# Two DMA queues for the KV stream of a decode block: V by SyncE, the next step's K by ScalarE

## The chip, the cores and the metric

One core of a Trainium2 chip runs the kernel; its other cores do nothing for it. The metric is the device time of one execution in microseconds (us). A core has TensorE (PE; its weight loads are shown apart as PEld), VectorE (DVE), ScalarE (ACT), GpSimd (POOL) and SyncE (SP, which only waits and issues), and 16 DMA engines that move data between the memory outside (HBM) and the on-chip SBUF. A DMA is issued by an engine, stands in that engine's DMA queue, and is cut into rows, one for each SBUF partition; with 128 partitions each of the 16 DMA engines carries eight rows of it.

## The reference, cut to what matters

One decode step for a batch of 2. `x` is normalised; an attention branch over a cache of 4096 positions is multiplied by a gate from a feed-forward branch and added to `x`:

```python
xn = _layernorm(x)                                   # (2, 1, 448)
q = (xn @ wq) -> (2, 16 heads, 1, 256)               # 16 query heads, 8 KV heads
scores = einsum("bhqd,bhkd->bhqk", q, k) * 256**-0.5 # k: (2, 8, 4096, 256), each KV head serves 2 query heads
o = einsum("bhqk,bhkd->bhqd", softmax(scores), v)    # v: the same shape as k
s = o.reshape(2, 1, 16 * 256) @ wo                   # (2, 1, 448)
g = silu(((xn @ w_gate) * (xn @ w_up)) @ w_down)     # inner width 1792
return x + s * g
```

All is float32. K and V are 67 MB each and are read once; with the weights the kernel reads 158.5 MB.

## The kernel before, in words

Batch and KV head make 16 steps; step `i` is head `i // 2`, batch `i % 2`. For one step K is 4 MB, laid out as 128 rows (partitions) of 32 KB, and so is V. The host joins V of step `i` and K of step `i + 1` into one tile `vk[i]` with rows of 64 KB (`ROW` = 8192 floats is one half of a row). These tiles go through `ring`, a pool of two SBUF buffers of 64 KB per partition. The weights go through `slot`, a pool with one buffer.

All large DMAs are issued by SyncE, at L68 in the helper `issue(n)`, which takes the next `n` transfers of a list `todo`. The list's order is written out by hand: `wq0` (half of wq), `first` (K of step 0, which takes a whole ring buffer), `vk[0]`, `wgu` (w_gate and w_up), `vk[1]`, `vk[2]`, `wd` (w_down), `vk[3]`, `vk[4]`, `wq1`, `vk[5]` to `vk[8]`, `wo`, `vk[9]` to `vk[13]`, then `last0` (K of step 15 and V of step 14, as two DMAs) and `last1` (V of step 15 and the last part of wo, as seven). A DMA into a buffer waits on SyncE until all that read the buffer's former contents is done, and what stands behind it on SyncE waits with it. Step `i` in the loop issues `vk[i + 2]`, whose buffer held `vk[i]`; before it, it issues the weight tile that is next, if one is due.

Ahead of the loop, the first three transfers are issued; ScalarE issues two small DMAs (`x`, L90, 3.5 KB, and `xo`, L94, 3.5 KB); VectorE normalises x (L107 to L117), and `xnT` is ready at L122. `query(0)` (L147, L150) multiplies it with `wq0`, VectorE transposes the result to `qT` (L159), `scores(0)` (L212) is computed from `first`, `issue(2)` follows (wgu and `vk[1]`), then `softmax` (L218 to L233) and `over` (L240 to L242).

The loop's body for step `i`, in program order, is this:

```python
        values(i, p[0], o)          # 32 matmuls on V of step i, L249
        ss = scores(i + 1)          # 32 matmuls on K of step i + 1, L212, and two maxima on VectorE, L213
        issue(1 + (i + 1 in weights))
        nc.scalar.activation(ob[...], o, AF.Copy, scale=p[1])     # L300
        p = softmax(*ss)            # VectorE, PE and two exponentials on ScalarE, L231
```

After four of the steps a piece of other work follows, when its weight tile is there: `ffn_in` (step 0, wgu), `ffn_out` (step 2, wd), `query(1)` (step 4, wq1), `project` (step 8, wo). These free the `slot` buffer for the next weight tile. Behind the loop come the last two steps, the rest of the projection (L276, L282), the gate and the addition (L351, L352) and the output's DMA (L353).

An engine runs its instructions in program order; Tile's semaphores hold an instruction back until what it needs is there. Below, `V3` is V of step 3 and `K4` is K of step 4; both are halves of `vk[3]`.

Of the kernel before, what the change touches and what calls it, by code (L numbers as in the profile page):

```python
# [22 lines left out]
ROW = 8192  # L23
# [14 lines left out]
def gated_decode_block(ctx: ExitStack, tc: tile.TileContext, x, xo, first, vk, last0, last1, wq, wo, wgu, wd, out):  # L38
    nc = tc.nc
# [7 lines left out]
    def bank(name="s", bufs=3):  # L47
        return psum.tile([128, 512], F32, name=name, bufs=bufs)
# [5 lines left out]
    loaded = {}  # L54
    todo = []

    def issue(n=1):
        for names, src, cuts in todo[:n]:
            weight = names[0].startswith("w")
            if weight:  # L60
                t = slot.tile([128, PART], F32, name="slot", align_bytes=512)
            else:
                t = ring.tile([128, 2 * ROW], F32, name="ring", align_bytes=512)
            width = ROW if not weight else PART // len(names)
            for i, name in enumerate(names):
                loaded[name] = t[:, i * width:(i + 1) * width]
            for lo, hi in zip(cuts, cuts[1:]):
                nc.sync.dma_start(t[:, lo:hi], src[:, lo:hi])  # L68
        del todo[:n]

    def plan(names, src, cuts=None):
        todo.append((names.split(), src, cuts or [0, src.shape[1]]))
# [8 lines left out]
    plan(f"k{LAST + 1} v{LAST}", last0, [0, ROW, 2 * ROW])  # L81
    plan(f"v{LAST + 1} wo2", last1, [0, 4096, 7168, *(ROW + i * D for i in (0, 2, 6, 7, 8))])
    issue(3)


    def early():
# [68 lines left out]
    def query(h):  # L155
        ps = bank()
        rows(ps, loaded[f"wq{h}"], 512)
        for r in range(REP):
            nc.vector.transpose(qT[h][:, :, :, :, r, :].rearrange("p b g d j -> p (g d) b j"),  # L159
                                ps[:, r * 256:(r + 1) * 256])  # L160
# [6 lines left out]
    def lift(ps):  # L167
        t = work.tile([128, D], F32, name="h")
        nc.scalar.copy(t, ps[:, :D])
        return t  # L170
# [6 lines left out]
    def ffn_in():  # L177
        pp = []
        for w in ("wg", "wu"):
            ps = bank()  # L180
            rows(ps, loaded[w], FC)
            pp.append(ps)
        g = work.tile([128, FC], F32, name="h")
        nc.scalar.copy(g, pp[0][:, :FC])
        h = work.tile([128, FC], F32, name="h")
        nc.vector.tensor_mul(h, pp[1][:, :FC], g)
        nc.vector.transpose(hT.rearrange("p i m -> p (i m)"), h)

    def ffn_out():
        ps = bank()  # L190
        for i in range(14):
            t = i % NT
            nc.tensor.matmul(ps[W * t:W * (t + 1), :D], hT[:, i], loaded["wd"][:, i * D:(i + 1) * D],
                             start=i < NT, stop=i >= 14 - NT)
        y = bank()
        spread(lift(ps), y, True, True)
        e = work.tile([128, D], F32, name="h")[:, :SL]
        nc.scalar.activation(e, y[:, :SL], AF.Sigmoid)
        nc.vector.tensor_mul(gate, y[:, :SL], e)


    def scores(i):
        g, b = divmod(i, B)
        k = loaded[f"k{i}"].rearrange("p (h d c n) -> p h d c n", h=2, d=2, c=NT)
        q = qT[g // 4][:, b, g % 4].rearrange("p d r j -> p d (r j)")
        m = work.tile([128, 4], F32, name="m")
        ss = []
        for h in range(2):
            s = bank()
            for d in range(2):  # L210
                for c in range(NT):
                    nc.tensor.matmul(s[W * c:W * (c + 1), :], q[:, d], k[:, h, d, c, :], start=d == 0, stop=d == 1)  # L212
            nc.vector.tensor_reduce(m[:, h:h + 1], s, axis=AX.X, op=OP.max)  # L213
            ss.append(s)
        return ss, m

    def softmax(ss, m):
        nc.vector.tensor_max(m[:, 2:3], m[:, 0:1], m[:, 1:2])  # L218
        sm = bank("sm", 1)
        nc.tensor.transpose(sm[:1, :128], m[:, 2:3], ident)  # L220
        mx = work.tile([1, NT, W], F32, name="mx", bufs=1)
        nc.vector.tensor_reduce(  # L222
            mx, sm[:1, None, :128].rearrange("p o (c j) -> p o j c", c=NT).to_broadcast([1, NT, W, NT]),
            axis=AX.X, op=OP.max)
        nc.tensor.transpose(sm[:, 128:129], mx.rearrange("p c j -> p (c j)"), one)  # L225
        nc.vector.tensor_scalar(m[:, 3:4], sm[:, 128:129], -1.0 / 16, None, op0=OP.mult)  # L226
        su = work.tile([128, 4], F32, name="su")
        pT = []
        for h in range(2):
            p = work.tile([128, 512], F32, name="p")  # L230
            nc.scalar.activation(p, ss[h], AF.Exp, bias=m[:, 3:4], scale=1.0 / 16, accum_out=su[:, h:h + 1])  # L231
            t = work.tile([128, 512], F32, name="pT", bufs=4)
            nc.vector.transpose(t, p)  # L233
            pT.append(t)
        return pT, su, sm

    def over(p):

        pT, su, sm = p
        nc.vector.tensor_add(su[:, 2:3], su[:, 0:1], su[:, 1:2])  # L240
        nc.tensor.matmul(sm[:, 130:131], add_head.rearrange("p a r j -> p (a r j)"), su[:, 2:3], start=True, stop=True)  # L241
        nc.vector.reciprocal(su[:, 3:4], sm[:, 130:131])  # L242
        return pT, su[:, 3:4]

    def values(i, pT, o, lo=0, hi=KB):

        for e in range(lo, hi):
            h, t, at = e // 8, e % NT, e % 8 * 2 * W
            nc.tensor.matmul(o[W * t:W * (t + 1), :], pT[h][:, at:at + 2 * W:2],  # L249
                             loaded[f"v{i}"][:, e * 512:(e + 1) * 512], start=e < NT, stop=e >= KB - NT)  # L250

    def combine(ob, n):

        cb = bank("cb", 1)
        src = ob.rearrange("p s (e d c k) -> p s e d c k", e=2, d=2, c=NT)
        for e in range(2):
            for c in range(NT):
                nc.tensor.matmul(cb[W * c:W * (c + 1), :n * 64], add_blocks[:, e].rearrange("p r j -> p (r j)"),  # L258
                                 src[:, :n, e, :, c, :], start=e == 0, stop=e == 1)
        return cb  # L260
# [6 lines left out]
    def turn(oT, cb, g, b, n):  # L267
        nc.vector.transpose(oT[:, g:g + n, :, :, DUP * b:DUP * (b + 1)].rearrange("p g d r j -> p (g d) r j"), cb)
# [4 lines left out]
    def project(oT, first, lo, hi):  # L273
        for i in range(lo, hi):
            t = i % NT
            nc.tensor.matmul(wide[W * t:W * (t + 1), :D], heads(oT, i, first),  # L276
                             loaded["wo"][:, i * D:(i + 1) * D], start=i < NT, stop=i >= LATE - NT)
# [11 lines left out]
    oT2 = const.tile([128, 1, 2, REP, W], F32)  # L289
    ss = scores(0)  # L290
    issue(2)
    p = over(softmax(*ss))
    for i in range(LAST):
        g, b = divmod(i, B)
        o = bank("o", 1)
        values(i, p[0], o)
        ss = scores(i + 1)

        issue(1 + (i + 1 in weights))
        nc.scalar.activation(ob[:, b * 4 + g if g < 4 else b * 3 + g - 4], o, AF.Copy, scale=p[1])  # L300
        if i == LAST - 1:
            cb = combine(ob, 6)
        p = softmax(*ss)
        if i < LAST - 1:
            p = over(p)
        if i == 7:
            cb = combine(ob, 8)
            for n in range(B):
                turn(oT0, cb[:, n * 256:(n + 1) * 256], 0, n, 4)
            ob = work.tile([128, 8, 512], F32, name="ob", bufs=1)  # L310
        if i in weights:
            if i == 0:
                ffn_in()
            if i == 2:
                ffn_out()
            if i == 4:
                query(1)
            if i == 8:
                project(oT0, 0, 0, EARLY)
# [6 lines left out]
    t = lift(wide)  # L326
# [71 lines left out]
```

## Time and profile before

| | |
|---|---|
| median of 3 runs | 377.5 us (377.33 to 377.6) |
| the profiled execution | 377.77 us, span 375.5 us |
| PE busy | 200.2 us, 53% of the span |
| PEld, DVE, ACT, POOL busy | 60.8, 72.4, 39.9, 1.2 us |
| SyncE's DMA queue (q1) | 158.54 MB, 97.9% of the span on 16 engines |
| ScalarE's DMA queue (q10) | 20 packets, 0.01 MB |
| instruction fetches (q8) | 11 packets, 0.18 MB |
| read from HBM | 158.54 MB, 422 GB/s over the span |
| granted TensorE clock, mean | 0.773 |

The page gives each engine's busy time, the span in 40 slices with the busy share in tenths, the DMA queues, and the chain of work that ended last. The trace behind it answers for single lines, stretches and DMA records. Times of day in it are microseconds from the start of the span. A row of the timeline is: start, duration, engine, line, operation, output and input, count, and in brackets how long the engine had been idle and what ended that.

### The profile page before, as it was taken

How to read it: one execution, taken by the hardware profiler on the slowest of the kernel's cores; microseconds unless marked ns; L12 is line 12 of the kernel's file. 1: busy time of each engine (PE TensorE's matmuls, PEld its weight loads, DVE VectorE, ACT ScalarE, POOL GpSimd, SP SyncE). 2: the span in 40 equal slices, each digit the busy share in tenths (PEclk: the TensorE clock that was granted, in tenths of full speed). 3: DMA queues.
4: the chain of work that ended last, by engine and by line, in shares of the span. 5: the costliest groups of instructions: out<-in, count | busy, mean ns of one | idle time of the engine just before them, and what ended most of it. 6: DMA issues, size and time to landing. Idle time of an engine off the chain costs nothing.

```text
span 375.5 us, 3325 instructions
## 1 busy us (share of the span) xinstructions
PE 200.2 (53%) x1440; PEld 60.8 (16%) x1440; DVE 72.4 (19%) x176; ACT 39.9 (11%) x87; POOL 1.2 (0%) x7
## 2 busy tenths in 40 slices
PE   0661648083752918539183758523637282809764
PEld 0110112021210202102021212100112121202222
DVE  3013040104030030300304031300212112210520
ACT  1001010001012020100101010100100101010220
POOL 1000000000000000000000000000000000000000
PEclk9966697667788776687867789765958685968999
DMA  8999999999999999999999999999999999999993
GB/s 334 438 471 391 436 452 447 447 435 389 429 440 442 447 403 443 440 447 426 442 434 440 433 416 408 463 447 433 435 440 421 440 426 419 442 412 436 415 417 139
DMA packets 4241, 158.74 MB, mean 423 GB/s; under 512 B 514, under 2 KB 772, under 8 KB 1156
## 3 DMA queue, kind: packets, MB, share of 16 engines
q1 hardware_dynamic: 4208, 158.54, 97.9%
q8 instruction: 11, 0.18, 0.2%
q10 hardware_dynamic: 20, 0.01, 0.0%
q14 instruction: 2, 0.02, 0.0%
HBM read 158.54 MB, written 0.01 MB: 422 GB/s over the span
## 4 chain that ended last, share of the span: by engine, by line
DMA 79%; PE 19%; SPq 1%; issue 0%; DVE 0%
DMA ring<-vk 68%; PE o L249 11%; PE s L212 8%; DMA ring<-last 6%; DMA ring<-first 5%; SPq L68 1%; PE acc L282 0%; DVE h L351 0%; DVE h L352 0%
## 5 line engine op out<-in xcount | busy, mean ns | idle before, releaser
L249 PE MATMUL o<-ring,pT 128*32 128x512 f32 x480 | 80.9, 835 | 85.4 <-DMA ring<-vk 84.8
L212 PE MATMUL s<-ring,qT 128*32 128x512 f32 x512 | 60.8, 616 | 3.4 <-DMA ring<-first 3.4
L213 DVE TENSOR_REDUCE m<-s 128x1 f32<-128x512 f32 x32 | 22.1, 691 | 209.1 <-PE s L212 209.0
L249 PEld LDWEIGHTS o<-ring,pT 128*32 128x32 f32 x480 | 20.1, 147 | 137.6 <-issue 110.9
L231 ACT ACTIVATE p<-s,m 128x512 f32<-128x512 f32 x32 | 21.7, 683 | 97.6 <-DVE m L226 97.6
L300 ACT ACTIVATE ob<-o,su 128x512 f32<-128x512 f32 x14 | 9.6, 688 | 196.0 <-PE o L249 196.0
L241 PE MATMUL sm<-su,add_head 128*128 128x1 f32 x32 | 8.6, 336 | 38.2 <-DVE su L240 38.2
L233 DVE STREAM_TRANSPOSE pT<-p 128x512 f32<-128x512 f32 x32 | 22.1, 711 | 15.7 <-ACT p L231 15.7
L212 PEld LDWEIGHTS s<-ring,qT 128*32 128x32 f32 x512 | 17.5, 114 | 43.4 <-issue 39.2
L147 PE MATMUL s<-slot,xnT 128*32 128x512 f32 (+1 forms) x96 | 16.9, 860 | 7.1 <-DMA slot<-wq 5.1
L241 PEld LDWEIGHTS sm<-su,add_head 128*128 128x128 f32 x32 | 7.2, 279 | 40.5 <-DVE su L240 40.3
L222 DVE TENSOR_REDUCE mx<-sm 1x128 f32<-1x512 f32 x16 | 10.8, 678 | 8.3 <-PE sm L220 8.3
L220 PE MATMUL sm<-ident,m 128*1 128x128 f32 x16 | 4.3, 269 | 15.1 <-DVE m L218 15.1
L225 PE MATMUL sm<-one,mx 1*128 1x1 f32 x16 | 3.5, 218 | 12.3 <-DVE mx L222 12.3
L276 PE MATMUL wide<-slot,oT 128*32 128x448 f32 x48 | 7.7, 797 | 0.0
L147 PEld LDWEIGHTS s<-slot,xnT 128*32 128x32 f32 x96 | 3.9, 150 | 16.2 <-issue 16.2
L231 ACT ACTIVATION_READ_ACCUMULATOR p<-s,m 128x1 f32 x32 | 6.3, 196 | 0.0
L220 PEld LDWEIGHTS sm<-ident,m 128*1 128x1 f32 x16 | 1.3, 79 | 29.1 <-issue 23.1
L258 PE MATMUL cb<-ob,add_blocks 128*32 128x64 f32 (+2 forms) x64 | 5.6, 476 | 0.3 <-ACT ob L339 0.3
L249 PE MATMUL wide<-ring,pT 128*32 128x512 f32 x32 | 4.2, 600 | 2.2 <-DMA ring<-last 2.2
L242 DVE RECIPROCAL su<-sm 128x1 f32<-128x1 f32 x16 | 2.7, 169 | 11.8 <-PE sm L241 11.8
L225 PEld LDWEIGHTS sm<-one,mx 1*128 1x128 f32 x16 | 2.1, 133 | 15.7 <-DVE mx L222 15.7
(57 smaller groups left out, 46.1 us busy)
## 6 DMA issues: line engine op xcount, KB each, us to landing
ring<-last SPq DMA_DIRECT2D x2, 4096.0 KB, 26.3
slot<-wq SPq DMA_DIRECT2D x2, 3584.0 KB, 23.5
slot<-wgu SPq DMA_DIRECT2D x1, 6272.0 KB, 38.8
slot<-wo SPq DMA_DIRECT2D x1, 5376.0 KB
ring<-first SPq DMA_DIRECT2D x1, 4096.0 KB, 20.5
slot<-wd SPq DMA_DIRECT2D x1, 3136.0 KB
ring<-last SPq DMA_DIRECT2D x1, 2048.0 KB
ring<-last SPq DMA_DIRECT2D x1, 1536.0 KB, 18.7
```

Source lines behind the costliest of these rows:

```text
L147: nc.tensor.matmul(ps[W * c:W * (c + 1), :n], xnT[:, k, :], block(NT * k + c), start=k == 0, stop=False)
L212: nc.tensor.matmul(s[W * c:W * (c + 1), :], q[:, d], k[:, h, d, c, :], start=d == 0, stop=d == 1)
L213: nc.vector.tensor_reduce(m[:, h:h + 1], s, axis=AX.X, op=OP.max)
L220: nc.tensor.transpose(sm[:1, :128], m[:, 2:3], ident)
L222: nc.vector.tensor_reduce(mx, sm[:1, None, :128].rearrange("p o (c j) -> p o j c", c=NT).to_broadcast([1, NT, W, NT]), axis=AX.X, op=OP.max)
L225: nc.tensor.transpose(sm[:, 128:129], mx.rearrange("p c j -> p (c j)"), one)
L231: nc.scalar.activation(p, ss[h], AF.Exp, bias=m[:, 3:4], scale=1.0 / 16, accum_out=su[:, h:h + 1])
L233: nc.vector.transpose(t, p)
L241: nc.tensor.matmul(sm[:, 130:131], add_head.rearrange("p a r j -> p (a r j)"), su[:, 2:3], start=True, stop=True)
L249: nc.tensor.matmul(o[W * t:W * (t + 1), :], pT[h][:, at:at + 2 * W:2], loaded[f"v{i}"][:, e * 512:(e + 1) * 512], start=e < NT, stop=e >= ...
L276: nc.tensor.matmul(wide[W * t:W * (t + 1), :D], heads(oT, i, first), loaded["wo"][:, i * D:(i + 1) * D], start=i < NT, stop=i >= LATE - NT)
L300: nc.scalar.activation(ob[:, b * 4 + g if g < 4 else b * 3 + g - 4], o, AF.Copy, scale=p[1])
```

## The change

Of each `vk` tile SyncE now issues only the V half, as a DMA of 128 rows of 32 KB. The K half goes on a list, and `issue_second()` issues it from ScalarE, into the same ring buffer. In the loop `issue_second()` stands behind the `ob` copy (L300) and ahead of the softmax; ahead of the loop it stands behind the two calls of `issue`, the first of which comes before ScalarE's DMAs of `x` and `xo`. Weights, `first`, `last0` and `last1` stay as they are. The layout in HBM is the same: each half row is read from the same 64 KB row as before.

```diff
+    second = []
+
+    def issue_second():
+        for t, src in second:
+            nc.scalar.dma_start(t[:, ROW:], src[:, ROW:])
+        second.clear()
+
     def issue(n=1):
         for names, src, cuts in todo[:n]:
...
             for i, name in enumerate(names):
                 loaded[name] = t[:, i * width:(i + 1) * width]
+            if names[0][0] == "v" and names[-1][0] == "k":
+                second.append((t, src))
+                cuts = [0, ROW]
             for lo, hi in zip(cuts, cuts[1:]):
                 nc.sync.dma_start(t[:, lo:hi], src[:, lo:hi])
         del todo[:n]
...
     issue(3)
+    issue_second()
...
     ss = scores(0)
     issue(2)
+    issue_second()
     p = over(softmax(*ss))
     for i in range(LAST):
...
         issue(1 + (i + 1 in weights))
         nc.scalar.activation(ob[:, b * 4 + g if g < 4 else b * 3 + g - 4], o, AF.Copy, scale=p[1])
+        issue_second()
         if i == LAST - 1:
             cb = combine(ob, 6)
         p = softmax(*ss)
```

## The prediction

> **What bounds the kernel now.** I read the page first: slices, queues, the chain.
>
> ```profile
> DMA  8999999999999999999999999999999999999993
> ...
> q1 hardware_dynamic: 4208, 158.54, 97.9%
> ...
> DMA 79%; PE 19%; SPq 1%; issue 0%; DVE 0%
> ```
>
> SyncE's queue q1 keeps the 16 DMA engines busy for 97.9% of the span. What is missing lies before the first row (about 2 us) and behind the last (some 5 us), not in the middle. So a transfer that arrives earlier shortens nothing by itself: the end moves only if the rows pass faster, or if the engines run dry. The chain's PE parts are covered by the next tile's transfer. Now the timeline, tile by tile (start, duration, what):
>
> ```profile
> 3.24 0.61 DVE L107 TENSOR_REDUCE st<-pT 2x1 f32<-2x448 f32 x1 [2.25 <-DMA pT<-x]
> 12.16 5.30 PE L147 MATMUL s<-slot,xnT 128*32 128x512 f32 x24 [5.09 <-DMA slot<-wq]
> ...
> 21.85 6.44 PE L212 MATMUL s<-ring,qT 128*32 128x512 f32 x32 [3.39 <-DMA ring<-first]
> ...
> 28.35 21.94 SPq L68 DMA_DIRECT2D ring<-vk  x2
> ...
> 189.24 6.37 PE L249 MATMUL o<-ring,pT 128*32 128x512 f32 x32 [4.80 <-DMA ring<-vk]
> ...
> 208.55 5.26 PE L249 MATMUL o<-ring,pT 128*32 128x512 f32 x32 [3.99 <-DMA ring<-vk]
> ...
> 227.84 3.64 PE L249 MATMUL o<-ring,pT 128*32 128x512 f32 x32 [1.86 <-DMA ring<-vk]
> ```
>
> Big tiles land every 19.3 us (208.55 - 189.24, 227.84 - 208.55), so half a tile is 9.65; `first`, also half, took 21.85 - 12.16 = 9.69. Line 28.35 shows that a ring buffer's next DMA is issued when the last `scores` on it ends. Third, how long PE holds a buffer, from the chain in order of time:
>
> ```profile
> 217.29 42.39 DMA ring<-vk
> 259.69 0.14 issue
> 259.82 5.22 PE o L249 x32
> 265.04 3.48 PE s L212 x32
> ...
> 298.43 6.39 PE o L249 x32
> 304.82 3.47 PE s L212 x32
> ```
>
> From landing to free buffer are 8.7 to 9.9 us; over the seven such pairs of the chain 8.55 to 9.86, mean 9.14. Last, single DMA records: a queue's share in a stretch, times 16 engines, times its length, is the time of the row that starts there.
>
> ```profile
> q10 hardware_dynamic: 1, 0.00, 15.6%
> ...
> q1 hardware_dynamic: 1, 0.03, 663.8%
> ```
>
> These are 10 ns each, at 5.56 and 5.59 us: a 448-byte row of `xo` on ScalarE's q10 (0.156 x 0.16 = 0.025 us), then the next q1 row of 28 KB on its engine, 1.062 us. The next answers are 20 ns each, at 322.14 and 323.06:
>
> ```profile
> q8 instruction: 1, 0.02, 291.9%
> ...
> q1 hardware_dynamic: 1, 0.07, 910.0%
> ```
>
> A 16 KB instruction fetch took 0.934 us, and the 64 KB row behind it 2.912 us, where most take 2.418.
>
> **The change part by part.** The profiled execution took 377.77 us: span 375.5 and 2.27 around it, 0.27 above the median 377.5. Terms are added to 377.77; the forecast is given against the median.
>
> *Rows of 32 KB.* The same bytes in twice the rows. Records give 1.213 us for 32 KB and 2.418 for 64 KB, so 2 x 1.213 - 2.418 = 8 ns per pair; 14 tiles x 8 rows per engine = 112 pairs, 0.9 us at most. But rows follow each other slightly closer than their records: the last half tiles landed 9.66 us apart (348.15, 357.81), against 9.65, and 28 x 0.01 = 0.3. I take 0.3, since landings set the end; the ends are 0 and 0.9.
>
> *Alternation of queues.* 14 K halves run beside a V half or a weight tile: 14 x 8 x 2 = 224 rows per engine that follow a row of the other queue. No row here shows two streams of full rows. Nearest is `xo`: the same two queues, the same kind of target. Its data, one q1 row and its semaphore write passed in turn on each of eight engines, and the q1 rows kept 1.062 us: 0. The far end is the row behind an instruction fetch: 2.912 - 2.418 = 0.5 us, 224 x 0.5 = 112 us, but that stream has another target. I take 0, and keep 0.04 us (9 us) as the range's upper bound; the far end stays outside as a rival. Below nothing: the rival on fetches.
>
> The Trainium skill ("DMA: Bandwidth & Descriptors", Issuing engines are not separate DMA queues) says that all issuers share 16 DMA engines and that issuing from several saves only sequencer time. By that rule this term is 0; the full DMA slices agree.
>
> *Order in the queues.* With rows in turn, both halves of a pair land together, 19.3 us after the pair starts, as today. But K overtakes wherever a weight tile stands before V. K2 then runs beside wgu, K3 beside V1, and V2 is alone. K4 runs beside wd, K5 beside V3, V4 alone; K6 beside wq1, K7 beside V5, V6 alone; K8/V7 and K9/V8 are together; K10 runs beside wo, K11 beside V9, and V10 alone. A lone V lasts 9.65 us. Behind V2 and V4 stand wd and wq1, already issued (cover; without it each would cost the following). Behind V6 and V10 the next pair is issued only when `scores` has freed the buffer. V10's last row ends 9.65 - 0.4 = 9.25 us after PE starts on V9 (0.4 from last row to PE: row end 40.72, PE 41.10). The pair's first row comes 9.14 us of PE work + 1.0 (issue 0.74 to first row 1.75) = 10.14 after. Engines idle 0.9 us; with the chain's 8.55 and 9.86, 0.3 to 1.6. At V6 the V of the pair before, first in its turns, lands one row (1.2 us) early, so -0.3, nothing. Which half goes first may swap, and the 0.9 with it, so I count it once; ends 0 and 1.6.
>
> *ScalarE issues 14 DMAs* at 0.33 to 0.85 us (SyncE's rows). In the loop the K issue stands behind the `ob` copy and waits for `scores` to end; behind it are the exponentials, which need that `scores` and then 2.5 us of DVE and PE (86.50 to 89.02). One issue fits: 0. If not covered, exp and thus the next `values` come 0.4 us late, with time to spare until its V lands (PE sat idle 4.80, 3.99 and 1.86 us before L249).
>
> *The start.* K1 now stands ahead of x and `xo` on ScalarE's queue and takes turns with wq0: 8 x (1.06 + 1.21) = 18.2 us after the first row (1.75, and 1.3 that the first rows took longer), so wq0 and x land near 22, where x came at 3.24. From there x's chain to xnT took 4.2 us (7.40): 26.2. `query(0)` takes 6.4 (12.16 to 18.5), the transposes to qT 0.9, `scores(0)` 6.5: V1/K2 are issued near 40.0 instead of 28.35. Cover: wgu is issued when `query(0)` ends, 32.6, its first row comes 1.0 later, and the rows before it (37.4 us of wq0, `first`, K1 and V0) last until 40.5; wgu then fills 15 us more. So 0; without those 6.9 us each later us of x is a us of the end.
>
> *The tail* (K15, V14, V15, wo2) stays on SyncE and is bound by its rows: 0.
>
> **Sum:** 0.3 + 0 + 0.9 + 0 + 0 + 0 = +1.2 us: 378.97 against the profiled execution, 378.7 against the median (+0.3%). Its own range: 0 to 0.9 and 0 to 1.6, so 377.5 to 380.0. A measurement here tells about 0.2% (0.75 us) from no change, so "same" is 376.75 to 378.25.
>
> **The rivals.**
>
> *Covered idle time.* The phase of the turns, or a transfer served whole before the other queue's, makes K land after V: with 9.65 us between them, `values` is done before K lands, and the buffer is free 3.5 us after it. No idle time: 377.5 + 0.3 = 377.8, the same. For: 0.9 us is a narrow miss. Against: `xo` shows a change after each row. The Trainium skill (same page, Queues, rings and completion order, Arbitration) states that an engine drains a packet, typically 9 to 17 descriptors, from a ring before it switches; a half tile is 8 rows per engine, so by that rule V would pass whole ahead of K, and the time would be this case's. The `xo` trace disagrees for small rows.
>
> *Each switch costs.* At 10 to 40 ns per row 224 rows give 2 to 9 us: 381 to 388; at 0.25 to 0.5 us, 56 to 112: 434 to 490. For: every row behind an instruction fetch is 0.5 us long. Against: the eight engines with `xo`.
>
> *Faster.* Each instruction fetch leaves its engine without data for (0.934 - 0.611) + 0.5 = 0.8 us (0.611 is a 16 KB row of V15). Twice it hit the engine that ends last: wgu came 1.45 us, V13/K14 1.5 us later than their rows add up to. If the second queue's rows fill those holes, -1.6 us: 377.5 + 0.3 - 1.6 = 376.2. It decides only if the idle time stays under 0.55 us. For: the other queue has rows waiting all through. Against: nothing here shows a hole being used; q10 was empty when they came.
>
> **How the numbers follow.** Forecast 0.45; covered idle time 0.22; each switch costs 0.22 (0.17 up to 388, 0.05 far above); faster 0.11. Slower by over 0.2%: 0.40 of the forecast's 0.45 + 0.22 = 0.62. Same: 0.22 + 0.05 = 0.27. Faster: 0.11. Range 376.2 to 386.0: from the faster case to 38 ns per switch; some 0.07 lies above it and 0.05 below. Cases of both signs hold chance; the likeliest's own is 377.5 to 380.0.
>
> **What would show it.** The DMA time of q1 and q10 together should stay near 98% of the span, q10 holding 14 x 4.19 = 58.7 MB. First `query` near 26 us, first `values` near 46, V2 and V10 alone; a DMA dent of under 2 us near 278 and none elsewhere. If K landings follow V by 9.65, transfers pass whole. If pairs of halves take over 19.4 us, switches cost. If the last `values` start over 1 us earlier with no dent, the holes were filled. The forecast is wrong if x's delay empties the engines before 41 us, or if rows beside the other queue differ from 2.42 us a pair.

## The result

The changed kernel takes 383.53 us at the median of six runs (381.66 to 383.77), the kernel before 377.33: a ratio of 1.0153, with an interval of 1.0141 to 1.0165. It is slower by 1.5%, where the prediction said 0.3%. The profiled execution took 383.56 us with a span of 381.4, 5.9 more than the span before. Lines of `kernel.py` have moved: `values` is L262, `scores` L225, SyncE's DMAs are L80, ScalarE's of K L63, and x's chain begins at L120.

The page of the changed kernel, DMA slices, queues and chain:

```profile
DMA  8999999999999999999799999999979999999994
...
q1 hardware_dynamic: 4208, 99.82, 61.3%
q10 hardware_dynamic: 2036, 58.73, 35.7%
...
DMA 59%; PE 24%; issue 7%; another core or an unknown queue 6%; DVE 2%; SPq 0%; ACT 0%; POOLq 0%; POOL 0%; ACTq 0%
```

Two sevens stand in a row of nines, in the slices around 186 and 281 us, and PE's share of the chain rose from 19% to 24%. A slice averages over 9.5 us; shorter windows (start and end; length, then the busy time of the engines; last the granted clock, DMA share, GB/s) show what is in them:

```profile
178.00:192.00 14.00, 9.78 (x66) 2.78 (x66) 2.38 (x5) 0.83 (x2) 0.00 (x0) 0.77 0.79 317
188.00:190.00 2.00, 1.21 (x12) 0.14 (x4) 0.94 (x3) 0.00 (x0) 0.00 (x0) 1.00 0.00 0
270.00:290.00 20.00, 11.96 (x80) 3.67 (x84) 3.97 (x9) 2.13 (x5) 0.00 (x0) 0.76 0.92 385
281.50:283.00 1.50, 0.63 (x8) 0.00 (x0) 0.77 (x2) 0.00 (x0) 0.00 (x0) 1.00 0.05 22
```

Between 188 and 190 us no row of data starts at all. The first stretch costs 14 x (1 - 0.79) = 2.9 us of all 16 engines, the second 20 x (1 - 0.92) = 1.6; summed record by record it is 2.9 and 1.8. The timeline around both has the waits that end them:

```profile
179.91 5.86 PE L262 MATMUL o<-ring,pT 128*32 128x512 f32 x32 [11.01 <-DMA ring<-vk]
...
189.26 0.33 SPq L80 DMA_DIRECT2D ring<-vk  x1
189.27 0.36 ACTq L63 DMA_DIRECT2D ring<-vk  x1
...
273.59 5.11 PE L262 MATMUL o<-ring,pT 128*32 128x512 f32 x32 [13.65 <-DMA ring<-vk]
...
282.19 0.33 SPq L80 DMA_DIRECT2D ring<-vk  x1
282.19 0.36 ACTq L63 DMA_DIRECT2D ring<-vk  x1
```

These are `values(5)` and, 3.5 us behind its end, when `scores(6)` is through, the issue of V7 and K8; then `values(9)` and the issue of V11 and K12. In each case K had gone ahead beside a weight tile (wq1, wo), only a lone V (V6, V10) was still in the queues (from 182 to 186 us all 58 rows that start are q1's), and it was through before PE freed the buffer for the next pair. When the queues fill again, the first rows are slow. The DMA answer for the 20 ns from 190.58 us on is:

```profile
q1 hardware_dynamic: 1, 0.03, 568.8%
```

That first row of V7 took 5.688 x 0.32 = 1.82 us instead of 1.21. Over the 16 engines this adds 0.7 us at the first stretch and 0.6 at the second.

In sum: DMA busy time of q1 and q10 rose from 97.9% of 375.5 us to 97.0% of 381.4, by 2.4 us (of it 0.9 for more rows and 1.3 for slow first rows), and the time without DMA work from 7.9 to 11.4, by 3.5. The stretches give 4.7 of idle time, so some 1.2 us less is idle elsewhere. Of that 0.7 is at the end (in the last 7.5 us the DMA share is 0.28, where it was 0.19). The rest fits a double count: by the records a row starts 3 to 4 ns before the one ahead of it on its engine ends, and there are 112 more rows per engine, 0.4 us in the sum of busy time.

### The profile page after: what moved, and what is told of

Read it like the earlier page. It is cut to its first block, busy times and chain, and to the rows that moved or that the text cites. A ratio compares the mean times of both kernels' runs of the same rounds, so it can differ in the third digit from the quotient of the medians.

```text
span 381.4 us, 3362 instructions
## 1 busy us (share of the span) xinstructions
PE 197.4 (52%) x1440; PEld 58.9 (15%) x1440; DVE 72.4 (19%) x176; ACT 39.9 (10%) x87; POOL 1.2 (0%) x7
## 4 chain that ended last, share of the span: by engine, by line
DMA 59%; PE 24%; issue 7%; another core or an unknown queue 6%; DVE 2%; SPq 0%; ACT 0%; POOLq 0%; POOL 0%; ACTq 0%
DMA ring<-vk 53%; PE o L262 12%; PE s L225 8%; DMA ring<-last 6%; PE wide L289 2%; PE s L160 1%; DVE pT L246 1%; SPq L80 0%; ACT p L244 0%; PE acc L295 0%; DVE m L226 0%; DVE mx L235 0%; PE s L163 0%; DVE qT L172 0%
## 5 line engine op out<-in xcount | busy, mean ns | idle before, releaser
L262 PE MATMUL o<-ring,pT 128*32 128x512 f32 x480 | 81.7, 843 | 62.7 <-DMA ring<-vk 62.7
L225 PE MATMUL s<-ring,qT 128*32 128x512 f32 x512 | 57.9, 592 | 0.9 <-DVE qT L172 0.9
L262 PEld LDWEIGHTS o<-ring,pT 128*32 128x32 f32 x480 | 19.9, 148 | 116.1 <-issue 100.0
L225 PEld LDWEIGHTS s<-ring,qT 128*32 128x32 f32 x512 | 16.5, 110 | 39.1 <-issue 33.1
L262 PE MATMUL wide<-ring,pT 128*32 128x512 f32 x32 | 4.2, 599 | 2.3 <-DMA ring<-last 2.3
```

## The experiments

Theory A: the loss sits in the two dry stretches, made by K overtaking V beside a weight tile. Theory B: rows of 32 KB are slow. Theory C: two queues side by side cost something on every row they share. Each kernel was timed beside the kernel before, whose median was 377.4 to 377.5 us.

**1. Halves on one queue.** The changed kernel, with

```diff
-            nc.scalar.dma_start(t[:, ROW:], src[:, ROW:])
+            nc.sync.dma_start(t[:, ROW:], src[:, ROW:])
```

> Both halves of each vk tile are issued by SyncE, one behind the other, as two DMAs with rows of 32 KB; ScalarE issues none of them. Theory A (the engines run dry twice, near 188 and 282 us, because K overtakes V beside a weight tile and leaves a lone V): nothing is overtaken here, so no dry stretch; only the rows' cost of 0 to 0.9 us, 377.3 to 378.3 us. Theory B (32 KB rows are slower than 64 KB rows by more than their records say): 381 us or more. Theory C (two queues share badly): 377.3 to 378.3 as with A.

Measured 378.29 us, a ratio of 1.0025 (1.0014 to 1.0035). Its page has nines all through:

```profile
DMA  8999999999999999999999999999999999999992
```

So half rows cost 0.9 us, the upper end of what had been worked out, and B is out as the cause of the other 5.

**2. x first.** `issue_second()` moved behind the DMAs of x and `xo`.

> As the changed kernel, but x and xo are issued by ScalarE ahead of K1. Theory A: the late x costs nothing, since wgu is issued in time and the engines stay full until after 180 us; the two dry stretches stay, 382.5 to 384.5 us. Rival (the late start of the first query is what the end pays for): 378 to 380 us.

Measured 383.19 us, 1.0154 (1.0136 to 1.0172). The first `query` started at 19.26 us instead of 27.93, and the end did not move: the late start of the compute is not paid for. The two dents are still there, as a seven and an eight in its DMA slices.

**3. Everything halved.** On top of 2:

```diff
-            if names[0][0] == "v" and names[-1][0] == "k":
-                second.append((t, src))
-                cuts = [0, ROW]
+            if len(cuts) == 2:
+                half = cuts[1] // 2
+                second.append((t, src, half))
+                cuts = [0, half]
...
-        for t, src in second:
-            nc.scalar.dma_start(t[:, ROW:], src[:, ROW:])
+        for t, src, half in second:
+            nc.scalar.dma_start(t[:, half:2 * half], src[:, half:2 * half])
```

> Every transfer up to vk13, the weights and first too, is issued as two halves side by side, the left by SyncE, the right by ScalarE; x and xo go first. Both queues then always hold the same tiles, and K can't overtake. Theory A: no lone V, no dry stretch, 377.5 to 379 us although more rows alternate than in the changed kernel. Theory C (each change of queue costs): worse than the changed kernel or equal, 383 us or more. With A the DMA slices show nines all through.

Measured 378.61 us, 1.0031 (1.0019 to 1.0043). The queues now share nearly everything:

```profile
DMA  8999999999999999999999999999999999999993
...
q1 hardware_dynamic: 4208, 86.48, 53.6%
q10 hardware_dynamic: 2900, 72.07, 44.5%
```

More rows alternate than in the changed kernel, and it is 4.9 us faster. It can't be told from experiment 1, which doesn't alternate at all. That is against C: sharing as such costs nothing that shows here, and what is left is that in the changed kernel the two queues held different things.

**4. Own buffers.** V and K get ring buffers of their own, with the overtaking left in:

```diff
+            elif names[0][0] == "v" and names[-1][0] == "k":
+                t = ring.tile([128, ROW], F32, name="vring", align_bytes=64)
+                u = ring.tile([128, ROW], F32, name="kring", align_bytes=64)
+                loaded[names[0]], loaded[names[1]] = t, u
+                second.append((u, src))
+                nc.sync.dma_start(t, src[:, :ROW])
+                continue
...
```

> As the changed kernel, but V and K have ring buffers of their own (two of 32 KB rows each in place of two of 64 KB), so the next V waits for values alone and no longer for the scores behind them. K still overtakes at the weight tiles. Theory A: V7 and V11 are issued 3.5 us earlier, which is more than the dry stretch before their first row, so both go: 377.5 to 379.5 us. Theory C: the queues share as before, 383 us.

Measured 379.21 us, 1.0049 (1.0032 to 1.0066). V7 is now issued when `values(5)` ends, 3.4 us before `scores(6)` does:

```profile
179.78 6.12 PE L274 MATMUL o<-vring,pT 128*32 128x512 f32 x32 [13.70 <-DMA vring<-vk]
185.71 3.62 PE L237 MATMUL s<-kring,qT 128*32 128x512 f32 x32
185.96 0.33 SPq L76 DMA_DIRECT2D vring<-vk  x1
189.40 0.33 ACTq L63 DMA_DIRECT2D kring<-vk  x1
```

The same overtaking with an earlier issue loses 1.8 us instead of 6; half of this is the rows' 0.9. By the records 0.2 us of idle time and 0.4 of slow first rows are left near 188 us: the cover is thin here.

**5 and 6. The second queue for one half of the steps.** In 5 K1 to K8 go through ScalarE and the later ones through SyncE; in 6 it is the other way round (`> 8`).

```diff
...
-                second.append((t, src))
-                cuts = [0, ROW]
+                if int(names[1][1:]) <= 8:
+                    second.append((t, src, nc.scalar))
+                    cuts = [0, ROW]
+                else:
+                    cuts = [0, ROW, 2 * ROW]
```

> K1 to K8 go through ScalarE as in the changed kernel; from K9 on K is issued by SyncE right behind its V, in rows of 32 KB. Theory A: the dry stretch before V7/K8 (near 188 us) stays with its 2.9 us and 0.7 of slow first rows, the one before V11/K12 (near 282, 1.8 and 0.6 us) is gone: 380.3 to 381.9 us. If a cost spread over all shared rows were behind it, some 8 of 14 parts of it would stay: 381 us, but with no dry stretch.

> K1 to K8 are issued by SyncE right behind their V; from K9 on K goes through ScalarE as in the changed kernel. Theory A: no dry stretch near 188 us, since no K overtakes there; the one behind wo, before V11/K12, stays (1.8 us idle and 0.6 of slow first rows, on top of 0.9 for the rows): 379.7 to 381.2 us.

Measured 380.61 us for 5 (1.0080, 1.0064 to 1.0096) and 380.42 for 6 (1.0082, 1.0067 to 1.0097). The slices of 5, then those of 6:

```profile
DMA  8999999999999999999799999999999999999994
```

```profile
DMA  8999999999999999999999999999979999999994
```

Each keeps one dent, the one that A named, and loses the other. Without the rows' 0.9 us they cost 2.3 and 2.1 us, together 4.4, where the changed kernel has 6.2 - 0.9 = 5.3. The 0.9 us between them is not shown to be a loss of its own: the runs of 5 are spread over 1.5 us and those of the changed kernel over 2.1, and by the records the stretch of 5 cost 3.0 us with its slow first rows and that of 6 2.7, together 5.7, where the two of the changed kernel cost 6.0.

**7. Weights on the second queue.** The tiles stay whole, rows of 64 KB, on SyncE; ScalarE issues wgu, wd, wq1 and wo.

```diff
-            nc.scalar.dma_start(t[:, ROW:], src[:, ROW:])
+            nc.scalar.dma_start(t[:, :src.shape[1]], src)
...
-            if names[0][0] == "v" and names[-1][0] == "k":
+            if weight and names != ["wq0"]:
                 second.append((t, src))
-                cuts = [0, ROW]
+                cuts = []
...
```

> The vk tiles are whole, rows of 64 KB, through SyncE as in the kernel before; ScalarE issues the weight tiles wgu, wd, wq1 and wo beside them, behind x and xo. Theory A: here too one queue overtakes the other, but what stays alone behind a weight tile is a whole tile of 19.3 us, about twice the time from landing to free buffer, so the engines never run dry: 377.0 to 378.2 us. Theory C (two queues side by side cost by themselves): 379 us or more.

Measured 377.57 us, 1.0005 (0.9996 to 1.0015): no difference. Two queues and overtaking, but with 19.3 us in the queue against some 9 of hold, cost nothing and gain nothing.

**8 and 9. A longer hold.** Half of the score matmuls are done twice, in the changed kernel (8) and in the kernel before (9).

```diff
-            for d in range(2):
+            for d in (0, 1, 0, 1)[2 * h:]:
```

> As the changed kernel, with half of the score matmuls done twice, some 1.74 us more of PE work between a tile's landing and its free buffer. Theory A: each of the two dry stretches gets 1.7 us longer, and nothing else does: 383.5 + 3.5 = 387 us (386 to 388.5). Theory C (the loss is spread over the shared rows): 383.5 us, as PE has time to spare elsewhere.

> As the kernel before, with the same extra score matmuls. All theories: the hold grows from 9.1 to 10.9 us against 19.3 us of the next tile's transfer, so it is hidden: 377.2 to 378.2 us.

Measured 377.64 us for 9 (1.0002, 0.9993 to 1.0012): the extra PE work is hidden. For 8 it was 385.94 (1.0217, 1.0185 to 1.0250), with runs from 384.0 to 387.0. That is 8.4 us above the kernel before, where the changed kernel has 6.2: 2.2 us more, not 3.5, and below the range that was expected. Its profiled execution, the slowest of the four at 387.0, shows one reason:

```profile
178.03 6.26 PE L262 MATMUL o<-ring,pT 128*32 128x512 f32 x32 [10.34 <-DMA ring<-vk]
...
189.49 0.33 SPq L80 DMA_DIRECT2D ring<-vk  x1
...
273.86 6.13 PE L262 MATMUL o<-ring,pT 128*32 128x512 f32 x32 [14.24 <-DMA ring<-vk]
...
285.20 0.33 SPq L80 DMA_DIRECT2D ring<-vk  x1
```

At the second stretch the hold is 285.20 - 273.86 = 11.3 us instead of 282.19 - 273.59 = 8.6, and by the records the engines idle 4.4 us instead of 1.8: as much more as the hold. At the first the hold grew by 2.1 (11.5 after 9.4), but V5 was there 1.9 us earlier, and the issue came only 0.2 us later; the idle time grew by 0.2. So the longer hold shows in full at the place where the landing stayed, and is nearly made up for at the one where it came earlier. Why V5 landed earlier there, and what the three faster runs did, isn't shown.

No version here beats the kernel before, whose DMA engines had nothing to gain between the first row and the last.

## Why the prediction was right or wrong

*What bounds the kernel, and the two places.* Right. The prediction had the DMA engines as the only bound, and named the lone V6 and V10 as the places where they can run dry. Experiments 3 to 6 show that these two make up most of the loss beyond the rows' 0.9.

*Order in the queues, +0.9.* This is the term that failed in size: 2.9 + 1.8 us idle and 0.7 + 0.6 of slow first rows, 6.0 in place of 0.9, as means over the 16 engines. Four parts of its working were off:

- It counted one dry stretch, and took the first for covered because V5 would land a row ahead of K7. By the records of the changed kernel V5's last row did end ahead of K7's on 12 of the 16 engines, but its semaphore (the 4-byte record that ends a transfer) came only behind K7's last row. On the other four engines V5 ended one or two rows behind K7, and the last of them, at 179.48 us, set its landing. A lead alone would not have covered the stretch: in the profiles of experiments 2 and 5 V5's rows led on every engine, by one to three rows, and the engines still idled 2.5 and 2.4 us there. Both places should have been counted.
- It took 16 engines for one. A landing is set by the last engine, but each of the others runs dry by its own end. From 186.85 to 190.2 us of the changed kernel the answer by queue has only V6's last rows and semaphores, and a fetch:

```profile
q1 hardware_dynamic: 19, 0.13, 9.3%
q8 instruction: 1, 0.02, 1.7%
```

  By the records ten engines had ended V6 between 186.8 and 187.3, the last four between 188.2 and 189.2, and V7's first row came at 190.2. From V6's last row to V7's first are 1.1 us, and 0.4 at the second stretch (282.74 to 283.14): that is what the sum's 0.9 speaks of, and the mean engine idled 2.9 and 1.8. The laggards' V5 had ended late too, and PE could start only at 179.91. The number of laggards fits the instruction fetches: four of 16 KB came before V6 ended (at 48.8, 92.3, 119.3 and 150.1 us). Each holds its engine for 0.9 us and makes the row behind it 0.5 us longer, 1.4 us in all: the engine that was last by 0.95 us when V0 landed was last by 2.37 at the next landing, behind the first of these fetches. Two more (at 218.9 and 258.3) came between the stretches, and at the second two engines were late. The prediction had the cause in hand, but counted 0.8 us for it, and in a rival alone.
- It left out that a tile's semaphore also waits for its turn. V9's last row ended at 271.85, but PE started on it at 273.59, 1.7 us later and not 0.4: on that engine a row of K11 (to 273.06) went in between, and V9's semaphore has its record at 273.05, where that row ends. The very `xo` records that the prediction read, data, one q1 row, then the semaphore, said so.
- It had no price for starting the engines again, 0.6 to 0.7 us each time. The first rows of the whole kernel, which took 1.3 us longer, were a row to take it from.

*Rows of 32 KB, +0.3.* Measured 0.9 (experiment 1), the upper end. The longer time between landings of the one pair of half tiles was too thin a base; the DMA records, at 8 ns a pair, gave the right figure.

*Alternation, 0.* Right. Two streams of full rows alternate at no cost that could be told: experiment 3 against 1 is 0.3 us, inside the intervals, and experiment 7 is the same as before. In a stretch of 5 us where both are at work, the answer by queue, from 200 to 205 us, is

```profile
q10 hardware_dynamic: 32, 1.05, 48.7%
q1 hardware_dynamic: 32, 1.05, 48.6%
```

The rule that the Trainium skill ("DMA: Bandwidth & Descriptors", Queues, rings and completion order) gives, a packet of typically 9 to 17 descriptors from one ring before the next has its turn, is not what these queues did: by the records rows of 32 KB took turns one by one, and V5 and K7 ended within two rows of each other on every engine. The rule that all issuers share the 16 DMA engines (same page, Issuing engines are not separate DMA queues) agrees with experiments 3 and 7: no gain in bandwidth from the second queue.

*ScalarE's issues, 0; the start, 0.* Right. V7 and K8 left at 189.26 and 189.27, well before the exponentials (191.85). And x came late as worked out:

```profile
23.71 0.61 DVE L120 TENSOR_REDUCE st<-pT 2x1 f32<-2x448 f32 x1 [22.72 <-DMA pT<-x]
...
27.93 4.20 PE L160 MATMUL s<-slot,xnT 128*32 128x512 f32 x24 [0.38 <-DVE xnT L135]
33.18 0.33 SPq L80 DMA_DIRECT2D slot<-wgu  x1
...
37.73 0.33 SPq L80 DMA_DIRECT2D ring<-vk  x1
```

23.71 for 22, wgu issued at 33.18 for 32.6, V1/K2 at 37.73 for 40.0. The engines stayed full, and experiment 2 shows that it cost nothing.

*The rivals.* Covered idle time is what experiment 4 comes to, and it brings most of the loss back. That each switch costs is refuted (3 and 7); 383.5 us lies among that rival's times (381 to 388), but by another cause. The stated range, 376.2 to 386.0, reached that far up for this rival alone; that it held the result is luck. The holes of the instruction fetches do not fill. One fetch came at 218.9 us, with rows of both queues at work; it took 0.93 us, and the row behind it on its engine, one of ScalarE's, was as much longer as in the kernel before. The answer for 20 ns from 219.80 us on is

```profile
q10 hardware_dynamic: 1, 0.03, 537.5%
```

which is 1.72 us in place of 1.21. The likeliest case's own range, 377.5 to 380.0, was too low by the four points above.

## What to carry to other kernels

When a second DMA queue takes half of a stream, ask not what the sharing costs but what each queue holds at every moment: a queue that carries extra tiles falls behind, the other runs ahead, and what stays behind it must still last longer than the buffer's hold plus the way from issue to first row. Work this margin out with the slowest engine's landing and the other engines' end, the semaphore's turn and the slow first rows, and count every place where it comes out near zero: here the place that the sum put at -0.3 us idled 2.9 on the mean of the engines. If two queues are wanted, split every transfer between them alike, or let the buffers of each queue come free by themselves. Neither gained anything here over one queue.

## What the runs showed of the hardware

- A DMA engine takes rows of two queues in turn, one by one, also at 32 KB, with no loss of rate that these runs could tell (32 rows of each queue in 5 us; 378.61 us with nearly everything shared, 378.29 with nothing shared).
- The semaphore that ends a transfer takes its turn like a row, so a tile can lie in SBUF for a row of the other queue, 1.2 us, before anybody is told.
- When the engines had run dry, 0.95 us passed from the issue to the first row, and the first rows took 1.8 to 1.9 us on average instead of 1.21.
- An instruction fetch of 16 KB sets the engine that it hits back by 1.4 us (0.93 for the fetch, 0.5 for the row behind it), also when a second queue has rows waiting.
- Rows of 32 KB instead of 64 KB, 112 more per engine, cost 0.9 us in 377.
